# Row-maximum scores twelve steps ahead instead of ten, a thinner lead, and cosine-matrix differences made by GpSimd during the first attention layer

## The chip, the cores and the metric

The kernel runs on one core of one Trainium2 chip. The metric is the device time of one execution in microseconds (us); the profiles are those of single executions on the chip. Engines are named as the profile names them: PE is the matrix engine (PEld its weight loads), DVE the vector engine, ACT the scalar engine, POOL is GpSimd, SP the engine that issues the DMAs here. Every DMA of this kernel is issued on SP's queue, in program order.

## What is computed

Four layers on one sequence of 2048 tokens with 640 features, float32: sliding-window attention (32 heads of 20, window 256), a Fourier mixing layer, the same attention again, the same Fourier layer again. Each adds its result to its input.

```python
def _A_ref(x, wqkv, wo):                      # x is layer-normalised
    q, k, v = ...                             # x @ wqkv, 32 heads of 20
    scores = einsum("bhqd,bhkd->bhqk", q, k) * 20 ** -0.5
    mask = (i - j >= 0) & (i - j < 256)
    p = softmax(where(mask, scores, -1e9))
    return concat(p @ v) @ wo
def _B_ref(x, Cr, Ci, Wr, Wi):                # x is layer-normalised
    a, b = x @ Wr.T, x @ Wi.T
    return Cr @ a - Ci @ b
x = x + A(norm(x)); x = x + B(norm(x)); x = x + A(norm(x)); x = x + B(norm(x))
```

The layers are called first attention, first Fourier, second attention, second Fourier below. Cr and Ci are the 2048 x 2048 cosine and sine matrices.

## The kernel before, in words

**Precision.** Most float32 products are made of three reduced-precision ones: each operand is cut into a high part (a copy by ACT) and a low part (source minus high part, by DVE or POOL), `split` at L224 and `cut_job` at L216.

**Attention, the heads loop (`heads`, L606).** The heads are taken as 8 quads of 4 heads; a quad has 16 blocks of 128 queries. That makes 128 steps, preceded by LEAD more. In the step numbered `step` the loop does three things for three different places:

- at s = step + LEAD, the scores of one query block with up to three key blocks, two heads at a time (`s_head`, matmul at L631). DVE adds the mask and takes the row maximum in one instruction (L636), into `mc`. Every fourth block, `m_rows` (L641) turns the maxima (L644), ACT negates them (L647), and two DMAs write them as rows 60 and 124 of `qp` (L649).
- at t = step, the same scores transposed with that extra row (`t_pair`, L659), so that PE delivers score minus maximum; ACT takes the exponential (L669), POOL clears the corners outside the window (`t_mask`, L675 and L679).
- at v = step - 1, probabilities times values (`pv`, L694), copied out at L701. The values carry a column of ones, so row 0 of each head's output is the sum; `finish` (L705) posts the DMA of the sums (L711), of the output (L712), the reciprocal on DVE (L714) and its store (L717), each some ticks later. A tick is half a step; the three delays are `at`, (2, 9, 11) before quad 7.

S and T scores share four PSUM banks before step -1, six after, handed out by `borrow`. A bank is free again once DVE (S) or ACT (T) has read it.

**What fills PE in the heads loop.** `fill(n)` runs about n rounds of other work. A round is one `yield 1` of `lockstep` (L244): two matmuls of 64 rows that run at once. First comes `project` (L568): chunks 2 to 9 of the q/k projection, 60 rounds each, 15 per half of a pair of 512-token blocks. While `self.lead` is true (step < -2) a chunk takes all four blocks at once in four banks (role "f", 6, 7, 4, 5), else two blocks in two banks (role "m", 6 and 7). A half ends with a small DVE read of its banks (L263). Finished blocks are copied out by ACT (L544) and cut by POOL jobs (L552, L211), stored (L524) and loaded again as `qp` and `kp` of a later quad (`pack`, L594) at due times counted in s. Before step -1 both halves of a step call `fill`, afterwards only the first. n is at least FIRST in the lead, RATE = 4 later. When the last chunk has begun its second half, `prepare(2)` (L927) loads the first outputs for the output projection; when the projection is over, `prepare(4)` (L944) posts loads of x into `big` (L952), and `partials` (L954) does 14 blocks of 18 rounds at LATE = 9 per step, as soon as the first set of outputs has been loaded, scaled (L892) and cut. Its first three parts need the sums of quads 0 to 5. A block ends with a DVE addition of the x that was loaded (L978).

**Lanes.** `job(lane, ...)` puts small instructions into a queue for ACT, DVE or POOL; each tick takes one from each lane (two in the lead). `flush(key)` issues those of a key at once.

**Fourier, the sequence part.** A Strassen-like scheme needs, of the first quarter (sb 0, part 0) of the matrices, three quarters-of-columns p, q, ... and three differences of them per row block j (8 blocks): q - p for the units "a1"/"a2", "b"/"b7" and "g". `load_to` (L1249) loads 1024 columns, `cut_to` (L1298) makes the difference (L1325 on DVE; L1336 on DVE, L1288 for the two "b7" units; L1345 on DVE for j < 3, else POOL) and cuts the operands; `seq` issues the matmuls (L1416). In the first Fourier layer `keep` (L1275) also stores each difference to `c_d` in HBM; in the second, `sums_kept` is true: it loads the difference (L1255, L1267) in place of the other half and makes none. These units begin while the last output blocks of the attention layer still run (`after_heads`).

## Time and the profile before

| | us |
|---|---|
| three runs | 2186.35, 2188.07, 2188.04 (median 2188.04) |
| the profiled execution, its own time | 2187.93 |
| its span, first to last instruction | 2186.2 |
| heads of the first attention, first S matmul to last T matmul | 125.0 to 528.8 |
| heads of the second attention | 1216.9 to 1617.8 |
| first Fourier, sequence matmuls (L1416) | 541.7 to 973.3 |
| second Fourier, sequence matmuls | 1628.8 to 2051.3 |

The groups of instructions by line give busy time and the mean of one instruction; the table of stretches gives busy time of each engine in stretches cut at chosen instants, with granted PE clock, share of the DMA engines' time and GB/s. In the profile a matmul's duration is longer than the distance between two starts, since matmuls overlap: what one costs is read from the starts.

### The profile page before, as it was taken

What the parts mean: (1) busy time and instruction counts of PE and PEld (TensorE: products, weight loads), DVE (VectorE), ACT (ScalarE), POOL (GpSimd) and SP (SyncE); (2) the same over time, 40 slices, a digit from 0 to 9 for tenths busy, and PEclk for the clock granted to TensorE, in tenths of its full rate; (3) what the DMA queues carried; (4) which work ended last, traced back from release to release, by engine and by line L of the source; (5) the groups of instructions that cost most, each with busy time, mean ns of one, the idle gap of its engine ahead of it and who ended that gap; (6) DMA issues with size and microseconds to landing.
All of it is one profiled execution on the core that took longest, in us unless ns stands there. A gap on an engine that the chain in (4) does not pass through costs nothing.

```text
span 2186.2 us, 48927 instructions
## 1 busy us (share of the span) xinstructions
PE 2118.1 (97%) x17872; PEld 1783.2 (82%) x17872; DVE 1603.7 (73%) x3931; ACT 1140.5 (52%) x2125; POOL 958.0 (44%) x1562
## 2 busy tenths in 40 slices
PE   7999999988999999999999999999899999999999
PEld 7987777677878888889999877776778888888899
DVE  6358888886897868786661588888767968677676
ACT  3117777656554545452341177777565645445332
POOL 3037776765614222322430377767655033231324
PEclk9999999999999999999999999999999999999999
DMA  5546666785555354656645556567855454546653
GB/s 183 175 157 190 198 180 215 211 224 169 202 192 189 127 183 141 214 177 207 207 156 167 162 186 200 181 212 226 216 161 182 140 182 132 174 152 208 222 165 125
DMA packets 227089, 398.40 MB, mean 182 GB/s; under 512 B 39969, under 2 KB 86561, under 8 KB 226849
## 3 DMA queue, kind: packets, MB, share of 16 engines
q1 hardware_dynamic: 226848, 395.28, 57.3%
q8 instruction: 141, 2.31, 0.5%
q14 instruction: 100, 0.81, 0.1%
HBM read 273.94 MB, written 120.06 MB: 180 GB/s over the span
## 4 chain that ended last, share of the span: by engine, by line
PE 78%; DVE 7%; DMA 5%; ACT 4%; issue 3%; POOL 2%; SPq 1%; ACTq 0%; DVEq 0%; POOLq 0%
PE banks L1416 29%; PE banks L239 15%; PE banks L257 12%; PE banks L694 6%; PE banks L659 5%; PE banks L1704 5%; PE banks L631 5%; DMA qp<-qk_d 2%; DVE banks L636 1%; ACT pt L669 1%; DMA x_d<-x 1%; PE banks L341 1%; DMA kp<-qk_d 1%; ACT big L1039 1%; DVE qp L232 1%
## 5 line engine op out<-in xcount | busy, mean ns | idle before, releaser
L636 DVE CUSTOM_DVE_ANT_0 banks<-banks,mask 128x384 f32<-128x384 f32 (+2 forms) x1024 | 527.6, 557 | 123.0 <-PE banks L631 99.9
L669 ACT ACTIVATE pt<-banks 128x768 f32<-128x768 f32 (+2 forms) x512 | 393.8, 772 | 168.7 <-PE banks L659 55.2
L675 POOL TENSOR_SCALAR_AFFINE_SELECT pt<-pt 128x256 f32<-128x256 f32 x512 | 213.3, 417 | 213.8 <-ACT pt L669 192.0
L257 PE MATMUL banks<-big,wc 64*128 64x512 f32 x1920 | 271.1, 394 | 0.4 <-DVE pt L442 0.4
L659 PE MATMUL banks<-qp,kp 61*128 61x384 f32 (+2 forms) x1024 | 210.2, 381 | 22.8 <-DVE mc L636 17.4
L694 PE MATMUL banks<-pt,vq 128*32 128x128 f32 x5760 | 211.6, 278 | 3.5 <-ACT pt L669 3.4
L631 PE MATMUL banks<-kp,qp 60*128 60x384 f32 (+2 forms) x1024 | 205.5, 347 | 6.7 <-DVE mc L636 3.1
L257 PEld LDWEIGHTS banks<-big,wc 64*128 64x128 f32 x1920 | 186.8, 185 | 22.6 <-ACT x L544 1.5
L679 POOL TENSOR_SCALAR_AFFINE_SELECT pt<-pt 128x256 f32<-128x256 f32 x448 | 193.8, 433 | 0.0
L226 ACT ACTIVATE qp<-pt 128x512 fp32r<-128x512 f32 (+1 forms) x200 | 123.2, 625 | 128.1 <-DVE pt L1347 51.7
L232 DVE TENSOR_TENSOR qp<-pt,qp 128x512 fp32r<-128x512 f32 (+1 forms) x198 | 156.6, 798 | 42.1 <-ACT qp L226 40.5
L694 PEld LDWEIGHTS banks<-pt,vq 128*32 128x32 f32 x5760 | 142.4, 110 | 51.5 <-issue 35.3
L659 PEld LDWEIGHTS banks<-qp,kp 61*128 61x128 f32 x1024 | 108.0, 184 | 87.3 <-DVE mc L636 65.2
L1416 PE MATMUL banks<-qp,big 128*128 128x512 f32 x648 | 152.9, 390 | 0.0
L631 PEld LDWEIGHTS banks<-kp,qp 60*128 60x128 f32 x1024 | 123.6, 186 | 31.9 <-DVE mc L636 16.4
L1345 POOL TENSOR_TENSOR pt<-pt,pt 128x512 f32<-128x512 f32 x32 | 47.2, 1475 | 231.4 <-DMA pt<-c 173.4
L226 ACT ACTIVATE c<-pt 128x512 fp32r<-128x512 f32 x146 | 90.4, 625 | 111.1 <-POOL pt L1325 57.1
L636 DVE DVE_READ_ACCUMULATOR2_ANT mc<- 128x1 f32 x1024 | 145.0, 142 | 0.0
L1416 PEld LDWEIGHTS banks<-qp,big 128*128 128x128 f32 x648 | 120.8, 188 | 24.2
L232 DVE TENSOR_TENSOR c<-pt,c 128x512 fp32r<-128x512 f32 x144 | 113.8, 793 | 26.9 <-ACT c L226 24.4
L1416 PE MATMUL banks<-qp,xc 128*128 128x512 f32 x480 | 117.4, 391 | 4.3 <-DVE xc L232 2.8
L552 POOL CAST c<-x 128x512 fp32r<-128x512 f32 x64 | 38.9, 611 | 166.5 <-ACT x L544 162.3
(253 smaller groups left out, 4479.9 us busy)
## 6 DMA issues: line engine op xcount, KB each, us to landing
pt<-c SPq DMA_DIRECT2D x166, 512.0 KB
qk_d<-c SPq DMA_DIRECT2D x80, 512.0 KB
kp<-qk_d SPq DMA_DIRECT2D x384, 80.0 KB
qp<-qk_d SPq DMA_DIRECT2D x384, 80.0 KB
kp<-u_d SPq DMA_DIRECT2D x32, 640.0 KB
o_d<-ou SPq DMA_DIRECT2D x64, 256.0 KB
x_d<-x SPq DMA_DIRECT2D x48, 320.0 KB
v_d<-pt SPq DMA_DIRECT2D x16, 768.0 KB
```

The lines of the kernel that those rows point to most:

```text
L226: nc.scalar.activation(hi, src, AF.Copy, scale=-1.0 if neg else 1.0)
L232: (eng or nc.vector).tensor_tensor(out=lo, in0=src, in1=hi.bitcast(F32), op=OP.subtract)
L239: self.nc.tensor.matmul(p, x, y, start=n == 0, stop=n == last)
L257: self.nc.tensor.matmul(ps[a], x[r], y[r], start=half + i == 0, stop=half == 1 and i == n - 1, skip_group_check=True)
L631: nc.tensor.matmul(p, qp[quad % 2][b:b + 60, z, qb * P:(qb + 1) * P], kp[quad % 2][b:b + 60, z, k0 * P:(qb + 1) * P], start=True, stop=True)
L636: nc.vector.tensor_tensor_reduce(out=p, in0=p, in1=self.mask[:, 384 - n * P:], scale=1.0, scalar=NEG, op0=OP.add, op1=OP.max, accum_out=mc ...
L659: nc.tensor.matmul(self.banks[:, banks[e], :n * P], kp[quad % 2][b:b + 61, z, kb * P:(kb + 1) * P], qp[quad % 2][b:b + 61, z, kb * P:(kb + ...
L669: nc.scalar.activation(pt[quad, kb][:, 2 * z:2 * z + 2, :n * P], self.banks[:, b0:b1 + 1, :n * P], AF.Exp, scale=SCALE)
L675: nc.gpsimd.affine_select(out=t[:, :, 0:P], in_=t[:, :, 0:P], pattern=[[0, 2], [1, P]], compare_op=OP.is_ge, fill=0.0, base=0, channel_mul ...
L679: nc.gpsimd.affine_select(out=t[:, :, 256:384], in_=t[:, :, 256:384], pattern=[[0, 2], [-1, P]], compare_op=OP.is_gt, fill=0.0, base=0, ch ...
L694: nc.tensor.matmul(self.banks[32 * h:32 * h + 32, bank, :P], vq[:, 96 * (kb % 4) + 21 * h:96 * (kb % 4) + 21 * h + 32], t[:, h, (qb - kb) ...
L1416: nc.tensor.matmul(self.banks[:, bk, :], p, b[q], start=start and m == 0, stop=stop and last and m == 2, skip_group_check=True)
```

## The change

Six edits. LEAD goes from 10 to 12 and FIRST from 7 to 5. In the projection only the first chunk of the lead takes four blocks at once. `differences_at`, called once a step in the first attention only (`self.ready == 0`), works through the 8 row blocks in turns of ten steps: in steps 0, 1, 2 of a turn three loads of 128 x 512 into the three `rr` tiles, in step 3 six POOL jobs of 128 x 256 that make the three differences in place, in step 7 the stores to `c_d` (at ticks 0, 2 and 4). The first Fourier layer then always loads the kept differences, as the second did; `keep`, its stores, `sums_kept` and the difference instructions of that quarter go. The delays in `finish` become (2, 12, 14) before quad 7, apart from the first block of quad 5. The staged cuts of the unit "b7" lose their first stage.

```diff
-LEAD = 10
+LEAD = 12
...
-FIRST = 7
+TURN = 10
+FIRST = 5
...
     def project(self):
         for c in range(2, NCH):
-            lead = self.lead
+            lead = self.lead and c == 2
...
+    def differences_at(self, step):
+
+        j, at = divmod(step, TURN)
+        if not (0 <= j < NB // 2 and self.ready == 0):
+            return
+        c = self.rr
+        if at < 3:
+            self.nc.sync.dma_start(c[at], self.a["c"][0, 0, j][:, at * 512:(at + 1) * 512])
+        elif at == 3:
+            for out, x, y in ((0, 1, 0), (1, 2, 1), (2, 2, 0)):
+                for cs in (slice(0, 256), slice(256, 512)):
+                    self.job("pool", "cd", lambda out=out, x=x, y=y, cs=cs: self.nc.gpsimd.tensor_tensor(
+                        out=c[out][:, cs], in0=c[x][:, cs], in1=c[y][:, cs], op=OP.subtract))
+        elif at == 7:
+            self.flush("cd")
+            for k in range(3):
+                self.post(2 * k, lambda k=k: self.nc.sync.dma_start(self.cd[k, j], c[k]))
...
-            at = (2, 9, 11) if quad < NQ - 1 else (1, 5, 6)
+            at = (1, 5, 6) if quad == NQ - 1 else (2, 9, 11) if (quad, bk) == (NQ - 3, 0) else (2, 12, 14)
...
             self.wide, self.lead, self.tiled = step + LEAD > steps, step < -2, step < steps - 1
+            self.differences_at(step)
...
-                self.post(3, lambda u=u: self.staged(u, 0, nc.vector))
-                self.post(6, lambda u=u: self.staged(u, 1))
-                self.post(9, lambda u=u: self.staged(u, 2))
+                self.post(6, lambda u=u: self.staged(u, 0))
+                self.post(9, lambda u=u: self.staged(u, 1))
...
     def kept_sum(self, u):
-        return self.sums_kept and self.order[u][:2] == (0, 0)
-
-    def keep(self, u, t):
-
-        sb, part, ph, j = self.order[u]
-        if not self.sums_kept and sb + part == 0:
-            kind = {"a1": 0, "b": 1, "b7": 1, "g": 2}[ph]
-            self.keeping.append(lambda: self.nc.sync.dma_start(self.cd[kind, j], t))
+        return self.order[u][:2] == (0, 0)
...
             if ph in ("a", "a1"):
-                eng = nc.vector if ph == "a1" else nc.gpsimd
-                if not self.kept_sum(u):
-                    eng.tensor_tensor(out=t1, in0=q, in1=p, op=OP.subtract)
-                    if ph == "a1":
-                        self.keep(u, t1)
+                if ph == "a":
+                    nc.gpsimd.tensor_tensor(out=t1, in0=q, in1=p, op=OP.subtract)
...
                 cut(q)
-                eng = nc.vector if self.order[u][:2] == (0, 0) and j < 3 else nc.gpsimd
                 if self.kept_sum(u):
                     t1, p = p, t1
                 else:
-                    eng.tensor_tensor(out=t1, in0=p, in1=t1, op=OP.subtract)
-                    self.keep(u, t1)
+                    nc.gpsimd.tensor_tensor(out=t1, in0=p, in1=t1, op=OP.subtract)
...
-        self.ready, self.hid, self.sums_kept = 8, False, True
+        self.ready, self.hid = 8, False
```

More of the change, by code (lines that the diff above doesn't have):

```diff
@@ L95, in __init__ @@
         self.cd = dram.tile([3, NB // 2, P, 512], F32, name="c_d")
-        self.sums_kept = False
         self.xs = [dram.tile([S, D], F32, name=f"x_d{i}") for i in range(3)]
@@ L1218, in take_fourier @@
         self.acc = {}
-        self.leaving, self.keeping = [], []
+        self.leaving = []
     def take_rest(self):
@@ L1272, in kept_sum, with staged @@
     def kept_sum(self, u):
-        return self.sums_kept and self.order[u][:2] == (0, 0)
-    def keep(self, u, t):
-        sb, part, ph, j = self.order[u]
-        if not self.sums_kept and sb + part == 0:
-            kind = {"a1": 0, "b": 1, "b7": 1, "g": 2}[ph]
-            self.keeping.append(lambda: self.nc.sync.dma_start(self.cd[kind, j], t))
-    def staged(self, u, stage, eng=None):
+        return self.order[u][:2] == (0, 0)
+    def staged(self, u, stage):
         j, out = self.order[u][3], self.cut_of.setdefault(u, [])
         p, q = cuts(self.raw_of[u], 512)
-        if stage == 0:
-            if not self.kept_sum(u):
-                eng.tensor_tensor(out=p, in0=q, in1=p, op=OP.subtract)
-                self.keep(u, p)
-            return
         c = self.ring.popleft()
         self.ring.append(c)
-        self.split(c[0], c[1], (q, p)[stage - 1])
+        self.split(c[0], c[1], (q, p)[stage])
         out.append(c)
-        if stage == 1:
+        if stage == 0:
             self.kept[j] = c
@@ L1307, in cut_to @@
                 if j:
-                    self.staged(u, 0, nc.gpsimd)
+                    self.staged(u, 0)
                     self.staged(u, 1)
-                    self.staged(u, 2)
                 continue
@@ L1322, in cut_to @@
             if ph in ("a", "a1"):
-                eng = nc.vector if ph == "a1" else nc.gpsimd
-                if not self.kept_sum(u):
-                    eng.tensor_tensor(out=t1, in0=q, in1=p, op=OP.subtract)
-                    if ph == "a1":
-                        self.keep(u, t1)
+                if ph == "a":
+                    nc.gpsimd.tensor_tensor(out=t1, in0=q, in1=p, op=OP.subtract)
                 src = [p] + ([t1] if ph == "a" else [])
@@ L1336, in cut_to @@
                     nc.vector.tensor_tensor(out=p, in0=q, in1=p, op=OP.subtract)
-                    self.keep(u, p)
                 src = [q, p]
@@ L1386, in seq @@
         sb, part, ph, j = self.order[n]
-        for f in self.keeping:
-            f()
-        self.keeping.clear()
         self.load_to(n + 3 + (ph == "a1" and len(self.raws) > 5))
```

## The prediction

> **What bounds the kernel now.** I read the page first, then the table of stretches cut at the stage borders, first attention and first Fourier beside their twins, then the groups and the timeline of the stages that the change touches.
>
> ```profile
> PE 2118.1 (97%) x17872; PEld 1783.2 (82%) x17872; DVE 1603.7 (73%) x3931; ACT 1140.5 (52%) x2125; POOL 958.0 (44%) x1562
> ...
> 125.00:160.80 35.80, 35.41 (x314) 28.86 (x313) 22.99 (x85) 5.60 (x12) 14.75 (x22) 1.00 0.46 149
> 160.80:412.90 252.10, 247.68 (x3491) 188.03 (x3489) 209.95 (x787) 184.21 (x335) 184.18 (x422) 1.00 0.64 196
> 412.90:427.80 14.90, 13.27 (x167) 8.52 (x163) 12.40 (x45) 8.70 (x19) 12.11 (x26) 0.81 0.67 213
> 427.80:501.20 73.40, 65.79 (x1011) 54.48 (x1007) 59.10 (x199) 42.47 (x76) 44.17 (x96) 0.99 0.79 218
> 501.20:541.70 40.50, 35.73 (x509) 29.93 (x504) 22.41 (x45) 26.83 (x52) 24.77 (x48) 1.00 0.53 159
> 541.70:670.40 128.70, 120.65 (x558) 97.45 (x557) 114.67 (x243) 71.92 (x146) 45.73 (x49) 0.99 0.59 194
> 670.40:973.30 302.90, 301.91 (x1330) 249.24 (x1330) 235.21 (x330) 159.02 (x297) 87.83 (x60) 1.00 0.52 168
> 1216.90:1252.10 35.20, 35.20 (x313) 30.00 (x313) 23.02 (x85) 5.60 (x12) 14.71 (x22) 1.00 0.46 152
> 1252.10:1504.30 252.20, 247.73 (x3495) 187.72 (x3491) 210.05 (x787) 184.41 (x336) 184.44 (x422) 1.00 0.63 197
> 1504.30:1517.50 13.20, 11.58 (x165) 7.43 (x161) 11.83 (x43) 8.56 (x19) 11.21 (x24) 1.00 0.81 247
> 1517.50:1590.40 72.90, 65.23 (x1009) 53.96 (x1009) 59.56 (x201) 42.53 (x76) 44.88 (x99) 1.00 0.82 216
> 1590.40:1628.80 38.40, 35.77 (x508) 29.96 (x505) 21.45 (x43) 26.87 (x52) 24.31 (x48) 1.00 0.47 146
> 1628.80:1748.40 119.60, 116.81 (x558) 98.78 (x557) 102.34 (x232) 74.43 (x150) 37.99 (x44) 0.99 0.52 166
> 1748.40:2051.30 302.90, 301.81 (x1330) 249.12 (x1329) 231.32 (x326) 157.45 (x292) 85.95 (x59) 1.00 0.51 167
> ```
>
> Columns of a stretch: length, busy time (and instructions) of PE, PEld, DVE, ACT, POOL, then granted clock, DMA share, GB/s. The seven stretches of a layer pair are the lead, steps 0 to 91 with projection, steps 92 to 96, steps 97 to 117, the rest up to the first sequence matmul, the first stretch of the Fourier sequence part and its remainder. PE sets the lead and the loop; DVE is close behind in the loop (209.95 of 252.10). The twins agree in the loop and in the remainder (302.90 both), and differ in the start of the Fourier part: 128.70 against 119.60. That pair is the best witness here, because the second Fourier layer already runs the code that the first one gets.
>
> **The change part by part.** The sum is made against the profiled execution's 2187.93, which is the median of the runs (2188.04) but for 0.1.
>
> *The lead.* How it is spent, from the timeline of PE:
>
> ```profile
> 138.87 0.34 PE L631 MATMUL banks<-kp,qp 60*128 60x384 f32 x2
> 139.05 1.77 PE L257 MATMUL banks<-big,wc 64*128 64x512 f32 x14
> 140.65 0.34 PE L631 MATMUL banks<-kp,qp 60*128 60x384 f32 x2
> ...
> L636 DVE CUSTOM_DVE_ANT_0 banks<-banks,mask 128x384 f32<-128x384 f32 x30 | 16.2, 583 | 7.7 <-PE banks L631 7.7
> ...
> L544 ACT ACTIVATE x<-banks 128x512 f32<-128x512 f32 x8 | 4.3, 595 | 27.7 <-PE banks L257 15.7 <-PE banks L631 12.0
> ```
>
> Fourteen matmuls, 7 rounds, take 140.65 - 139.05 = 1.60, so a round is 0.229, and a pair of S matmuls 0.18. A step of the lead is now 15 rounds and two pairs, 3.79; with FIRST = 5 it is 10 rounds and two pairs, 2.65. (Five divides a half of 15 into three fills; the due times ask for at most 4.8 rounds per step.) Eight steps of 3.79 become ten of 2.65: 30.3 to 26.5, a gain of 3.8; steps -2 and -1 and the two transposes of maxima stay. DVE needs 4 x 0.58 = 2.3 of a 2.65 us step, so it doesn't take over, but it is near. Against the gain stands the two-bank form of the second chunk: the next pair of blocks must wait in the same banks for ACT's copies (0.595 each), and each half for DVE's small read, which queues behind two reductions. There are three such borders in the new lead, which no T or PV covers there; I bound them by 0 and 2.2 (one copy for 0.6 and its start, twice most of a reduction), and take 1.0. Per attention -2.8, together **-5.6**.
>
> *Where the 20 rounds go.* The lead now does 115 rounds instead of 135. At RATE 4, with halves of 15 taken as 4, 4, 4, 3, the remaining 345 rounds fill 92 steps; 365 fill 97.
>
> ```profile
> L257 PE MATMUL banks<-big,wc x22: 386/392/394, 404.8 to 411.3; 64*128 64x512 f32 x22
> L257 PE MATMUL banks<-big,big x18: 299/306/465, 428.6 to 430.0; 64*128 64x320 f32 x18
> ```
>
> The rows show the last projection matmul (step 91) at 411.3 and the first of the output projection (step 97) at 428.6: five steps with no fill, waiting for the outputs of quad 5's first block, the block whose early reciprocal the change keeps. They run at 13.20 / 5 = 2.64 a step, since DVE is busy 11.83 of 13.20; steps with projection take 252.20 / 92 = 2.74. So 20 rounds, 4.6 us of PE, move under DVE's cover for 5 x 0.1 = 0.5 an attention, **+1.0**. If that cover were not there, they would cost 4.6 each and the lead would be worth nothing.
>
> *The end of S.* S ends at step 116 instead of 118. From step 118 on a step is shorter:
>
> ```profile
> 1590.40:1611.20 20.80, 19.62 (x329) 15.79 (x325) 9.47 (x18) 15.86 (x30) 16.23 (x34) 1.00 0.42 128
> ```
>
> 20.80 / 7 = 2.97 against 72.90 / 21 = 3.47, though some of that average is single waits. Two steps at -0.3: **-1.2** for both attentions (0 to -2).
>
> *Loads in quad 7.* PE's waits in the two output stretches (first attention, then second), and a load of x by the chain of waits:
>
> ```profile
> PE banks L631 <- DMA kp<-qk_d: 1.0, 1, 1.0
> ...
> PE banks L631 <- DMA qp<-qk_d: 2.0, 1, 2.0
> ...
> 1589.56 3.97 DMA big<-x_d
> ```
>
> The first S of quad 7 waits for its operands, issued at steps 96 to 99 behind the first outputs and stores that crowd SP's queue. With LEAD 12 they go out at 94 to 97, ahead of the output loads of step 98. I take half, **-1.5** (-3.0 to 0). The other way goes the load of x: `prepare(4)` is posted when projection ends, at step 92 now, at 97 then. I count the jobs of the POOL lane to the first set of outputs as ready one step later, so block 0 runs in steps 98 and 99, and its addition on DVE (L978) is due about 6 us after the issue. Landing takes 3.97 plus SP's backlog; behind the waiting addition stand the reductions of S, and PE behind them. **+1.0** (0 to +6).
>
> *The clock.* In the five empty steps the first attention shows a granted clock of 0.81 and 14.90 us, its twin 1.00 and 13.20; steps 97 to 117 add 0.5. At most -2.2 if filled steps keep the clock; the twin had the same empty steps at full clock, so I take half, **-1.1**. The Trainium skill ("TensorE: Matmul & The Clock Gate", "What's actually happening") says that an idle window of about 3.4 us halves the clock, on a window that runs free of the kernel. That would explain why one of two equal stretches fell to half; by that rule alone the whole 2.2 is gained and the sum is 1.1 lower.
>
> *First Fourier.* What goes, from the stretch 541.7 to 670.4 (two DVE groups, one POOL group) and the stores:
>
> ```profile
> L1336 DVE TENSOR_TENSOR pt<-pt 128x512 f32<-128x512 f32 x6 | 4.1, 685 | 0.0
> ...
> L1345 DVE TENSOR_TENSOR pt<-pt,pt 128x512 f32<-128x512 f32 x3 | 2.1, 686 | 0.0
> ...
> L1345 POOL TENSOR_TENSOR pt<-pt,pt 128x512 f32<-128x512 f32 x2 | 3.6, 1804 | 5.4 <-DVE c L232 5.4
> ...
> L1280 SPq DMA_DIRECT2D c_d<-pt x18: 319/326/423, 539.4 to 663.0; - x18
> ```
>
> Removed are 24 differences and 24 stores; the loaded bytes stay, in other pieces. PE there is idle 128.70 - 120.65 = 8.0 against 2.8 in the twin. The twin differs by 9.1 in this stretch and by 2.1 in the one before it, where the first differences are made and one ACT wait falls that need not belong. I take **-10.0** (-9.1 to -11.2).
>
> *GpSimd in the first attention.* POOL's groups in the loop, one step of it, and DVE's wait for the sums:
>
> ```profile
> L675 POOL TENSOR_SCALAR_AFFINE_SELECT pt<-pt 128x256 f32<-128x256 f32 x153 | 62.2, 406 | 59.6 <-ACT pt L669 55.5 <-PE banks L694 2.6 <-PE banks L659 0.9
> L211 POOL TENSOR_TENSOR c<-x,c 128x256 fp32r<-128x256 f32 x40 | 29.6, 739 | 0.0
> ...
> 259.25 0.41 POOL L675 TENSOR_SCALAR_AFFINE_SELECT pt<-pt 128x256 f32<-128x256 f32 x1
> ...
> 261.11 0.86 PE L694 MATMUL banks<-pt,vq 128*32 128x128 f32 x24
> ...
> DVE rc L714 <- DMA sm<-ou: 0.2, 1, 0.2
> ```
>
> 48 subtractions of the form of L211 are 48 x 0.739 = 35.5 us, over 80 steps in which POOL is idle 27% (59 us). But they come six in three steps: 4.4 us against 3 x 0.74 = 2.2 idle, so POOL falls up to 2.2 behind and catches up in the other seven. The mask ends at 259.66 and the last third of PV that needs it starts near 261.7: a margin of 2.0. The projection's own POOL jobs (six every eight steps) share the lane, one job a tick, so two groups in a row add up; I take **+1.0** (0 to +6: 0.8 a turn). The 48 DMAs are 16 us of SP (0.33 each by L1280) in 219, and about 58 GB/s beside 196; the kernel moves 247 in the stretch at 1504. Their loads wait for stores three steps back; the stores wait for POOL, with the loads of later quads behind them, which are needed some five steps later. The later reciprocals I cost at nothing: DVE waits 0.2 for the sums in the whole loop (last row), and only quad 5's first block feeds a wait.
>
> The Trainium skill ("SBUF — State Buffer", "SBUF: two separate sides") has a rule against this part: GpSimd and a DVE operation with two SBUF inputs exclude each other for a whole instruction. The reductions (0.583) read PSUM and one SBUF operand, so by the rule only DVE's few weight cuts would wait, at most 10 x 0.74 = 7.4 us of DVE, and the sum would be up to 7 higher; no run here shows it for these.
>
> Sum: -5.6 + 1.0 - 1.2 - 1.5 + 1.0 - 1.1 - 10.0 + 1.0 = -16.4, so 2187.9 - 16.4 = **2171.5**.
>
> **The rivals.**
> - *Only the Fourier part pays.* The borders in the lead, DVE in steps 92 to 96 and the wait for x eat the heads' gain: -10 + 1 gives **2179**. For it: DVE has only 0.35 us a step to spare in the new lead. Against it: PE is the only full engine there.
> - *Everything pays.* No bubbles (-7.6 for the lead), +1.0, -2.0, -3.0, -2.2, -11.2, no charge for POOL: -25 gives **2163**.
> - *The differences don't leave the bound.* If the twins differ for another reason (their loads, the clock), only the heads' -6.4 with POOL's and part of the 9.1 remain: **2180**. Against it: the twin runs the very code.
> - *Slower: POOL becomes the bound of steps 3 to 6 of every turn.* PV waits for the masks behind the subtractions. With all 35.5 us on the path it is 2171.5 - 1 + 35.5 = **2206**. It decides once the delay exceeds the margin of 2.0 by more than 17.4 / 8 = 2.2 us a turn, twice the backlog that I count.
>
> **How the numbers follow.** Forecast 0.50, only Fourier 0.20, everything 0.12, differences 0.08, slower 0.10. All but the last are faster; 0.2% (4.4 us, about what a measurement tells from no change) is missed by the upper ends of the second and fourth, 0.06 together: faster 0.84, same 0.06, slower 0.10. The range 2162 to 2184 holds the first four with their bounds; the forecast's own is 2166 to 2177.
>
> **What would show it.** The lead (first S to first T matmul) at 32 to 34 instead of 35.2 to 35.8. Projection matmuls up to step 96 and at most one or two steps without fill. In the first Fourier stretch about 119.6 to 121, with no difference on DVE or POOL. Steps 3 to 6 of a turn in the first attention within 0.2 of the second's; if its steps 0 to 91 are over 6 longer than the twin's, POOL's cost is wrong. PE waits at quad 7's start shorter; a wait of L978 for the load of x near step 99 if that term is larger. A clock below 1 in the filled steps would show that the empty ones didn't cause it.

## The result and the profile after

The changed kernel takes 2210.74 us (median of 4 runs, 2210.48 to 2211.21) against 2187.19 (4 runs, 2186.24 to 2188.07): ratio 1.0111, 95% interval 1.0097 to 1.0126. It is 23.6 us slower; the prediction said 16.4 faster. The profiled execution took 2210.48.

The page's busy line and the table of stretches of the changed kernel, cut at the same borders as before (lead, steps 0 to 91, 92 to 96, 97 to 117, the rest, first stretch of the Fourier part; the second attention below):

```profile
PE 2123.2 (96%) x17872; PEld 1787.0 (81%) x17872; DVE 1587.6 (72%) x3913; ACT 1140.6 (52%) x2125; POOL 976.7 (44%) x1604
...
123.70:158.70 35.00, 32.98 (x282) 25.95 (x281) 27.38 (x101) 4.38 (x10) 12.30 (x18) 1.00 0.52 168
158.70:438.10 279.40, 258.36 (x3497) 193.33 (x3494) 215.21 (x784) 183.60 (x334) 213.03 (x467) 0.96 0.69 214
438.10:452.90 14.80, 13.81 (x204) 10.45 (x200) 12.39 (x45) 9.67 (x20) 12.03 (x24) 1.00 0.84 254
452.90:531.90 79.00, 66.00 (x985) 53.52 (x981) 56.25 (x186) 43.47 (x81) 46.27 (x102) 0.96 0.77 216
531.90:570.60 38.70, 36.41 (x520) 31.13 (x521) 19.67 (x43) 26.59 (x50) 25.52 (x50) 1.00 0.48 148
570.60:689.40 118.80, 115.90 (x559) 97.66 (x558) 102.49 (x232) 74.40 (x151) 37.39 (x44) 1.00 0.51 169
...
1234.50:1268.90 34.40, 32.78 (x282) 25.89 (x281) 27.40 (x101) 4.38 (x10) 12.30 (x18) 1.00 0.53 168
1268.90:1520.40 251.50, 246.78 (x3495) 187.17 (x3493) 210.06 (x784) 183.49 (x334) 182.58 (x419) 1.00 0.62 191
1520.40:1534.20 13.80, 13.50 (x202) 10.33 (x198) 12.14 (x44) 9.63 (x20) 11.94 (x24) 1.00 0.82 233
1534.20:1613.50 79.30, 67.51 (x985) 54.81 (x981) 56.35 (x186) 43.51 (x81) 46.44 (x103) 0.94 0.81 212
```

The first Fourier layer gave what it should: 118.8 against 128.7. Two stretches cost far more than that. Steps 0 to 91 of the first attention take 279.4 against 252.1, while the second attention, which makes no differences, takes 251.5. Steps 97 to 117 take 79.0 and 79.3 against 73.4 and 72.9, in both attentions. POOL is busier by its subtractions (213.03 against 184.18) and still idle for a quarter of the stretch.

**Steps 0 to 91.** PE's waits there, before (4.3 us in all):

```profile
PE banks L659 <- DVE mc L636: 3.4, 10, 0.6
PE banks L659 <- DMA qp<-qk_d: 0.9, 3, 0.4
```

A row gives who waits for whom, the sum in us, how often, and the longest. PE's two largest in the changed kernel, then two of POOL's:

```profile
PE banks L712 <- POOL pt L693: 8.1, 5, 2.5
PE banks L649 <- DVE mc L654: 4.6, 2, 4.3
```

```profile
...
POOL rr L617 <- DMA rr<-c: 9.3, 6, 3.4
POOL rr L617 <- DMA kp<-qk_d: 9.0, 2, 5.1
```

PE waits for POOL, for which it had no wait before, and for DVE up to 4.3 us at a time, where 0.6 was the longest. The first chain, in POOL's timeline, PE's and SP's:

```profile
289.23 0.72 POOL L617 TENSOR_TENSOR rr<-rr,rr 128x256 f32<-128x256 f32 x1 [5.10 <-DMA kp<-qk_d]
289.91 0.41 POOL L693 TENSOR_SCALAR_AFFINE_SELECT pt<-pt 128x256 f32<-128x256 f32 x1
```

```profile
290.37 0.41 PE L712 MATMUL banks<-pt,vq 128*32 128x128 f32 x4 [2.53 <-POOL pt L693]
```

```profile
285.81 0.40 SPq L613 DMA_DIRECT2D rr<-c  x1
```

A subtraction (L617) stood 5.10 us in POOL's in-order queue for its second block, whose load SP issued only at 285.81 (its row names a packed load that signals on a semaphore for which the subtraction also waits). The masks stood behind it, and PE's probabilities times values (L712) behind the masks. The second chain, in DVE's timeline, POOL's at the same time, and PE's:

```profile
332.56 5.10 DVE L211 TENSOR_TENSOR wc<-x,wc 128x384 fp32r<-128x384 f32 x1
337.58 0.55 DVE L654 CUSTOM_DVE_ANT_0 banks<-banks,mask 128x384 f32<-128x384 f32 x1
```

```profile
332.42 0.74 POOL L211 TENSOR_TENSOR c<-x,c 128x256 fp32r<-128x256 f32 x1
333.11 0.40 POOL L693 TENSOR_SCALAR_AFFINE_SELECT pt<-pt 128x256 f32<-128x256 f32 x1
...
336.52 0.72 POOL L211 TENSOR_TENSOR c<-x,c 128x256 fp32r<-128x256 f32 x1
```

```profile
333.62 0.34 PE L677 MATMUL banks<-qp,kp 61*128 61x384 f32 x2
338.25 0.69 PE L649 MATMUL banks<-kp,qp 60*128 60x384 f32 x2 [4.29 <-DVE mc L654]
```

A low part of a weight cut, 0.64 us on average before, took 5.10. It began while POOL worked off a backlog without a gap, and it ended 0.4 us after POOL's last instruction (336.52 + 0.72 = 337.24). The nine instructions that POOL started meanwhile are masks and pieces of the projection; no difference is among them. The reductions of S stood behind it on DVE, their banks stayed full, and PE stopped. PE's stop cut off the exponentials, hence the masks, and that is how POOL ran dry at last.

The longer stalls have an echo. Windows around a PV stall of 1.7 us that ended at 228.8, granted clock in the third column from the right:

```profile
222.00:230.20 8.20, 6.50 (x87) 4.85 (x87) 5.00 (x17) 5.46 (x10) 3.73 (x10) 1.00 0.81 211
230.20:233.60 3.40, 2.93 (x30) 1.78 (x30) 2.25 (x9) 1.50 (x3) 1.89 (x4) 0.51 0.66 157
233.60:242.00 8.40, 8.40 (x115) 6.38 (x119) 6.76 (x26) 5.78 (x10) 8.40 (x19) 1.00 0.49 156
```

For 3.4 us PE has half its clock and starts 30 matmuls where the next rate (115 in 8.4 us) would give 47. Steps 0 to 91 hold four such stretches of 3.4 us and one of 6.8. In these 20.4 us PE is busy for 17.7, so the half clock costs some 9 us (an estimate: half of the busy time), next to 15.7 of added waits (all rows of PE's waits in these steps sum to 20.0, against 4.3). The Trainium skill ("TensorE: Matmul & The Clock Gate", "What's actually happening") has the clock halved after an idle window of about 3.4 us. The trace agrees on the length, as every halved stretch in these steps is one or two such windows. It differs on the idle time: the halved stretches lie on one grid of 3.41 us, and each follows a stretch of the grid in which PE stood idle for 1.70 us or more, about half of it. With up to 1.47 us idle the next one kept the full clock. Idle time is not all that counts: at 1537.5 us the clock was halved after a stretch with 0.46 us of it.

**Steps 97 to 117.** One of PE's waits in the first attention, SP's timeline (issues of DMAs), and one window:

```profile
...
PE banks L649 <- DMA qp<-qk_d: 5.8, 2, 3.2
```

```profile
467.62 0.53 SPq L878 DMA_DIRECT2D x<-o_d  x1
468.58 0.52 SPq L884 DMA_DIRECT2D rr<-r_d  x1
469.60 0.35 SPq L735 DMA_DIRECT2D r_d<-rc  x1
470.44 0.39 SPq L524 DMA_DIRECT2D qk_d<-c  x1
471.97 0.34 SPq L971 DMA_DIRECT2D big<-x  x1
472.52 2.05 SPq L594 DMA_DIRECT2D qp<-qk_d  x3
...
478.53 1.24 SPq L594 DMA_DIRECT2D qp<-qk_d  x3
```

```profile
465.00:475.00 10.00, 9.77 (x163) 8.13 (x164) 7.30 (x29) 6.37 (x12) 6.83 (x17) 1.00 1.00 254
```

The DMA engines are full (1.00). Output loads, loads of x and the projection's last stores stand among the packed loads of quad 7's second block. Its scores at step 104 wait, and the step takes 11.4 us (11.1 in the second attention). Before, step 104 took 4.55, and step 106, where these scores ran then, 3.6.

### The profile page after: what moved, and what is told of

It is laid out like the page before. It is cut to its first block, busy times and chain, and to the rows that moved or that the text cites. A ratio compares the mean times of both kernels' runs of the same rounds, so it can differ in the third digit from the quotient of the medians.

```text
span 2208.8 us, 48983 instructions
## 1 busy us (share of the span) xinstructions
PE 2123.2 (96%) x17872; PEld 1787.0 (81%) x17872; DVE 1587.6 (72%) x3913; ACT 1140.6 (52%) x2125; POOL 976.7 (44%) x1604
## 4 chain that ended last, share of the span: by engine, by line
PE 70%; DMA 8%; DVE 8%; ACT 4%; issue 3%; POOL 3%; SPq 3%; ACTq 0%; DVEq 0%; POOLq 0%
PE banks L1412 29%; PE banks L239 13%; PE banks L257 10%; PE banks L1700 5%; PE banks L712 5%; PE banks L677 4%; PE banks L649 3%; DMA kp<-qk_d 2%; DVE banks L654 2%; DMA qp<-qk_d 1%; DMA kp<-u_d 1%; SPq L594 1%; ACT pt L687 1%; DMA qk_d<-c 1%; PE banks L341 1%
## 5 line engine op out<-in xcount | busy, mean ns | idle before, releaser
L693 POOL TENSOR_SCALAR_AFFINE_SELECT pt<-pt 128x256 f32<-128x256 f32 x512 | 212.4, 415 | 206.0 <-ACT pt L687 184.6
L257 PE MATMUL banks<-big,wc 64*128 64x512 f32 x1920 | 280.5, 399 | 3.6 <-DVE seen L263 1.9
L649 PE MATMUL banks<-kp,qp 60*128 60x384 f32 (+2 forms) x1024 | 207.8, 349 | 20.4 <-DMA qp<-qk_d 14.1
L712 PE MATMUL banks<-pt,vq 128*32 128x128 f32 x5760 | 215.6, 279 | 10.1 <-POOL pt L693 8.1
L712 PEld LDWEIGHTS banks<-pt,vq 128*32 128x32 f32 x5760 | 144.5, 110 | 62.4 <-issue 35.1
L697 POOL TENSOR_SCALAR_AFFINE_SELECT pt<-pt 128x256 f32<-128x256 f32 x448 | 190.2, 424 | 0.0
L232 DVE TENSOR_TENSOR c<-pt,c 128x512 fp32r<-128x512 f32 x146 | 118.4, 814 | 26.5 <-ACT c L226 24.1
L1329 POOL TENSOR_TENSOR pt<-pt 128x512 f32<-128x512 f32 x30 | 42.3, 1413 | 165.8 <-DMA pt<-c 141.9
```

The costliest lines, as they stand in the source:

```text
L232: (eng or nc.vector).tensor_tensor(out=lo, in0=src, in1=hi.bitcast(F32), op=OP.subtract)
L257: self.nc.tensor.matmul(ps[a], x[r], y[r], start=half + i == 0, stop=half == 1 and i == n - 1, skip_group_check=True)
L649: nc.tensor.matmul(p, qp[quad % 2][b:b + 60, z, qb * P:(qb + 1) * P], kp[quad % 2][b:b + 60, z, k0 * P:(qb + 1) * P], start=True, stop=True)
L693: nc.gpsimd.affine_select(out=t[:, :, 0:P], in_=t[:, :, 0:P], pattern=[[0, 2], [1, P]], compare_op=OP.is_ge, fill=0.0, base=0, channel_mul ...
L697: nc.gpsimd.affine_select(out=t[:, :, 256:384], in_=t[:, :, 256:384], pattern=[[0, 2], [-1, P]], compare_op=OP.is_gt, fill=0.0, base=0, ch ...
L712: nc.tensor.matmul(self.banks[32 * h:32 * h + 32, bank, :P], vq[:, 96 * (kb % 4) + 21 * h:96 * (kb % 4) + 21 * h + 32], t[:, h, (qb - kb) ...
```

## The experiments

All are compared with the kernel before, run beside them on the same chip (medians 2186.2 to 2188.3).

**One half of the change at a time.** The first keeps the differences and undoes the heads' edits (LEAD 10, FIRST 7, four blocks throughout the lead, old delays in `finish`); the second is the kernel before with the heads' edits.

> The differences alone: GpSimd makes them in the first attention's heads, the first Fourier layer reads them; lead, projection and reciprocals as before. Theory L (the subtraction stands in POOL's queue before its operands have landed, and the masks behind it hold PE): first attention 15 to 25 us longer than before in steps 0 to 91, first Fourier 11 to 12 shorter, no long step 104; about 2187.2 + 20 - 11.5 = 2196, 2190 to 2202. Rival H (the stalls of the first attention come from the heads' new timing, not from the differences): steps 0 to 91 within 3 us of before, about 2176.

> The heads' edits alone (LEAD 12, FIRST 5, four blocks only for the first chunk, later reciprocals); the differences are made in the first Fourier layer as before. Theory J (DMAs crowd at steps 97 to 101, where the end of the projection, the first output loads and the loads of quad 7 now meet): step 104 takes about 11 us in both attentions, each attention 5 to 8 us longer from step 92 on and 0.8 shorter in the lead; about 2187.2 + 10 = 2197, 2193 to 2202. Rival: the long step 104 is a late effect of the differences' DMAs; then it is about 3.5 us here and the kernel 2184 to 2187.

The differences alone took 2202.49 (ratio 1.0067, 1.0044 to 1.0090), the heads' edits alone 2195.11 (1.0036, 1.0023 to 1.0050): each half slows the kernel. With the differences alone steps 0 to 91 take 279.1; with the heads alone they take 251.5, and step 104 takes 10.1 and 11.8. So the two losses have separate causes, and their sum, 14.8 + 7.4, is near the change's 23.6.

Theory L came near in time, not in mechanism. PE's largest wait in steps 0 to 91 with the differences alone:

```profile
PE banks L677 <- DMA qp<-mt: 9.6, 6, 3.4
```

These are late rows of maxima; the masks held PE for only 3.3 us. With scores twelve steps ahead no such wait is left, the masks hold PE for 8.1, and the loss is the same 27 us.

**When the subtractions run, and their loads.**

```diff
-        elif at == 3:      # e3: subtractions two steps later, stores at 8, one tick apart
+        elif at == 5:
...
-        if at < 3:         # e4: loads in the first turn only
+        if at < 3 and j == 0:
```

> As after, with the subtractions put into POOL's lane at step 5 of a turn instead of 3, the stores at step 8 instead of 7. Theory L: POOL no longer waits for loads, most of the 21 us of quads 1 to 5 go; about 2210.7 - 17 = 2194, 2189 to 2199. Rival W (POOL's work, 4.4 us in three steps, is too much beside the masks): the work is as dense as before, 2207 to 2212.

> As after, but the three loads are made in the first turn alone: POOL subtracts and stores in all eight turns, what it stores is not the differences from the second turn on. Theory L: POOL never waits for a load after the first turn, quads 1 to 5 within 5 us of before; 2210.7 - 18 = 2193, 2187 to 2197. Rival W: the work is all there, 2206 to 2211.

Two steps more for the loads gave nothing: 2210.3 (1.0112, 1.0085 to 1.0139), steps 0 to 91 279.9. PE's waits for the masks went, others came. Without the loads it was 2197.39 and 263.8; what remained were two stalls, 3.9 us behind a DVE cut and 3.5 behind ACT. My theory of late loads alone had fallen.

**Loads and stores without subtractions; subtractions spread; DVE's cuts given to GpSimd.**

```diff
-                    self.job("pool", "cd", ...)   # e5: none; e6: one a step, TURN = 11
...
-                self.cut_job("dve", ("w", c), ...)
+                self.cut_job("pool", ("w", c), ...)   # e7
```

> The changed kernel without the six GpSimd subtractions of a turn: the three loads and three stores stay, so what is stored are blocks of the matrix and not their differences, and the first Fourier stage computes with those. The changed kernel took 2210.7 us, its first attention 279.4 us from step 0 to step 91 against 252.1 before. Theory P (GpSimd's work does the harm: where two subtractions fall into a step, its four masks of 0.40 us and two subtractions of 0.72 us are 3.0 us in a step of 2.7; it goes without a pause from instruction to instruction, DVE's subtraction of a weight cut, which reads two operands in SBUF as GpSimd's do, then waits up to 5.1 us, the masks come late, and TensorE's clock is halved for 7.7 us after each stall): steps 0 to 91 fall to 252 to 256, no cut on DVE lasts over 1.5 us, time 2184 to 2189. Rival D (the 0.8 MB of loads and stores a turn hold up SP's queue and the packed loads): steps 0 to 91 stay over 268, time over 2199.

> The changed kernel with one subtraction a step, at the third to the eighth step of a turn, a turn of 11 steps, and the stores at the ninth. Theory P: a step then has 1.6 us of masks, 0.72 of a subtraction and at most one piece of a projection's cut, 3.0 us at the worst and mostly 2.3; the backlog is shorter and rarer, and some stalls go: steps 0 to 91 at 258 to 270, time 2190 to 2202. Rival Q (GpSimd's in-order queue waits for the loads whatever the spacing, as SP issues them late): no gain, time over 2206, POOL's waits for the matrix's loads as in the changed kernel (9 us from 158 to 480).

> The changed kernel with the low parts of the projection's weights subtracted by GpSimd in place of DVE, as two halves each. Starvation (the 5.1 us cut of 332.6 was DVE waiting until GpSimd ran dry): no DVE subtraction is left that reads two operands in SBUF while the subtractions run, so that stall of 4.3 us and the halved clock behind it go, about 8 us, less what GpSimd's longer queue adds to late masks: 2199 to 2206. Rival (the long cut only shows a jam that has another cause): a stall of DVE or a wait for a mask takes its place, 2208 to 2216.

(The 7.7 us of halved clock in the first of these texts was misread; the windows show 3.4 or 6.8.) Theory P failed in part: without any subtraction the time is 2203.34 and steps 0 to 91 take 272.1, three quarters of the loss. No cut on DVE lasts over 1.1 us there; ACT waits, by the same kernel's waits of ACT in those steps:

```profile
ACT ou L714 <- DMA o_d<-ou: 15.5, 9, 2.9
...
ACT mt L660 <- DMA qp<-mt: 4.9, 7, 1.4
```

ACT may not write its next output or row of maxima until the last one has been stored, and these stores come late. PE in turn waits for ACT, in two rows that the kernel before doesn't have:

```profile
PE banks L644 <- ACT pt L682: 4.7, 15, 0.6
PE banks L672 <- ACT ou L714: 4.7, 8, 1.5
```

All of PE's waits come to 13.3 us there, 9.0 more than before, and 3.4 us at half clock are 1.7 more. The rest of the 20 us lies in matmuls that count as busy; how it is lost isn't shown. Spreading the subtractions gave 2208.02, with three stalls for masks of up to 5.6 us behind subtractions that waited for loads, so rival Q came nearer. With the cuts on GpSimd it was 2208.47. The long DVE cut was gone, as starvation demands, but masks took its place (11.0 us, longest 5.0), and the rival's time came. In the second attention, which makes no differences, the same edit gained: 33.5 us for the lead and 249.7 for steps 0 to 91, against 34.4 and 251.5.

**The parts one by one.** Loads alone (stores moved ahead of the heads), stores alone, both on buffers of their own, both with half the bytes, subtractions alone (loads in the first turn, stores ahead of the heads).

> The changed kernel without the subtractions and with the matrix's blocks loaded in the first turn only: 24 stores of 256 KB are left in the first attention's steps; what is stored isn't the differences. With loads and stores steps 0 to 91 took 272.1 us, with none of it (the heads' edits alone) 251.5. If the traffic itself or each place in SP's queue costs, half of it costs about half: 258 to 265, time 2194 to 2200. If it takes loads and stores together (SP held up by a load that waits for the store of the same buffer), 251 to 255 and 2190 to 2193.

> The changed kernel without the subtractions and with the stores moved ahead of the heads (of the first block, eight times over; what is stored isn't the differences): 24 loads of 256 KB are left in the first attention's steps, nothing waits for them, and a load waits for no store. By traffic or places in SP's queue alone, about half of the 20.6 us of loads and stores together: steps 0 to 91 at 258 to 265. If it takes both, 251 to 255. The time itself also holds what the moved stores cost ahead of the heads.

> The changed kernel without subtractions, with the 24 loads and the 24 stores of the first attention's steps on buffers of their own: loads go into two of the three, stores come from the third, so that no load waits for a store's landing; what is stored isn't the differences. Loads alone gave 255.2 us for steps 0 to 91, stores alone 254.1, both on the same buffers 272.1, none 251.5. Theory W (both cost more than their sum because each load waits in SP's queue for the store of its buffer, and packed loads, output stores and row loads wait behind it): 256 to 260. Rival T (12.6 MB are simply too much beside the heads' own traffic of 197 GB/s): 268 to 274.

> The changed kernel with the 48 subtractions in the steps, but with loads in the first turn only and the stores ahead of the heads; what is stored isn't the differences. Subtractions and stores together gave 263.8 us for steps 0 to 91, in two stalls. If GpSimd's work costs by itself (DVE's subtraction held until GpSimd pauses, and the halved clock after it), one or two stalls stay, at least one behind a DVE subtraction of over 4 us: 256 to 264. If it harms only by holding up the stores in SP's queue: 251 to 254.

> The changed kernel without subtractions, with 24 loads and 24 stores in the first attention's steps as before, but each of half a block (128 KB in place of 256); the full stores lie ahead of the heads; what is stored isn't the differences. Loads and stores of whole blocks gave 272.1 us for steps 0 to 91 (270.8 on buffers of their own), loads alone 255.2, stores alone 254.1. If the bytes do it (6.3 MB then, as with loads alone or stores alone): 253 to 258. If the 48 places in SP's queue do it (some 0.45 us each, 21 us, on a queue that issues for 187 of 250 us): 265 to 272.

| left in the first attention's steps | steps 0 to 91, us | time, us |
|---|---|---|
| nothing (heads' edits alone) | 251.5 | 2195.11 |
| 24 stores | 254.1 | 2188.04 |
| 24 loads | 255.2 | 2187.56 |
| loads and stores | 272.1 | 2203.34 |
| the same, buffers apart | 270.8 | 2202.80 |
| the same, half the bytes | 265.5 | 2196.00 |
| 48 subtractions | 257.9 | 2189.48 |
| subtractions and stores | 263.8 | 2197.39 |
| all (the change) | 279.4 | 2210.74 |

Each stretch is from one profile, each time a median. In the second attention, where these kernels do the same, steps 0 to 91 take 251.1 to 251.7, so 2.6 us are clear of that spread. The times don't compare with the first row's as the stretches do, since there the first Fourier layer still makes the differences. In the rows of the 24 loads, of half the bytes and of the 48 subtractions, stores of whole blocks lie ahead of the heads.

Loads cost 3.7, stores 2.6, both 20.6: neither costs half of what both do, as traffic or places alone would have it. Theory W falls, since separate buffers change 1.3 us, and rival T has its range. Half the bytes in as many transfers take away 6.6: at the edge of the range for places in SP's queue, and far from that for bytes (253 to 258). The subtractions alone cost 6.4, and nearly all of it is one stall. This was expected if GpSimd's work costs by itself. DVE's timeline of that kernel:

```profile
317.86 4.84 DVE L211 TENSOR_TENSOR wc<-x,wc 128x384 fp32r<-128x384 f32 x1
322.63 0.55 DVE L669 CUSTOM_DVE_ANT_0 banks<-banks,mask 128x384 f32<-128x384 f32 x1
```

Here no load and no store of a difference is about, and the cut again ends only when POOL runs dry: nine POOL instructions start during it. PE loses 3.89 us, and from 321.7 on it has half its clock for 6.8. Four kernels have one cut each of 4.7 to 4.8 us (this one, the differences alone, later subtractions, first loads only), besides the change's 5.10. In all five POOL starts nine instructions during it without a gap, and the cut ends 0.4 us after the last.

**Another queue for loads and stores.**

```diff
-            self.nc.sync.dma_start(...)
+            self.nc.scalar.dma_start(...)
```

> As with the loads and stores on buffers of their own and no subtractions (steps 0 to 91 270.8 us), but the 24 loads and 24 stores of the first attention's steps are issued by ACT's queue in place of SP's; bytes and times in the program are the same; what is stored isn't the differences. Half the bytes in as many transfers still gave 265.5. If SP's queue, which then has 48 places of 0.45 us less, is what the steps wait for: 252 to 258 and 2188 to 2193, ACT bearing 21 us of issuing in its idle time. If the bytes on the DMA engines are, or ACT has no room either: 264 to 274.

A miss of both ranges: 2242.3 (1.0247, 1.0214 to 1.0280), steps 0 to 91 309.9. ACT's waits there:

```profile
ACT mt L660 <- DMA qp<-mt: 20.6, 13, 3.9
ACT ou L714 <- DMA o_d<-ou: 19.8, 10, 4.1
ACT ou L714 <- DMA qp<-qk_d: 9.3, 2, 5.2
```

The last row is odd, as an output copy needs no packed load. In the trace each transfer of these kernels signals on one of eight semaphores, taken in turn (240 or 241 transfers on each in the kernel before), and none is issued before the transfer eight places ahead of it has landed: all updates of a semaphore by one transfer lie ahead of the issue of the next one on it. ACT's queue shares the eight, so ACT itself stood still for SP's transfers. The run therefore doesn't settle bytes against places. It points to eight in flight as a limit of its own. So does SP's largest wait in the kernel with loads and stores on SP's queue, where packed loads wait for a block of the matrix that they don't need:

```profile
SPq L594 <- DMA rr<-c: 7.9, 12, 1.5
```

In the steps before, 434 transfers in 249.6 us (the starts of steps 0 and 91) at a mean of 3.56 us from issue to landing, the last update of the transfer's semaphore, are 6.2 in flight. With loads and stores, 473 at 3.79 us would be 7.2 if the steps kept that length. A queue that full is held up by each burst, which fits the jump from 3.7 and 2.6 to 20.6, and fits that half the bytes took only 6.6 of it. That is worked out, not tested: no run here allows more than eight. Nor do SP's waits for transfers grow as the loss does: they sum to 17.6 us with neither, 28.4 with loads alone and 32.7 with both.

**Step 104.** The heads' edits with FIRST 7, so that projection ends at step 83; and with the old reciprocals.

> The kernel before with the change's edits of the heads (scores twelve steps ahead, the lead projecting one chunk with all four blocks, later reciprocals), but with the old rate of 7 fills in the lead, so that 50 rounds more lie in the lead and the projection ends at step 83 in place of 96. With the rate of 5 it took 2195.1, and step 104 took 10.1 and 11.8 us, waiting for the seventh quad's packed loads. Theory X (the four loads of x, the last stores of the projection and the loads of the output projection, which all start when the projection ends, meet that quad's packed loads at steps 97 to 101): with the end 13 steps earlier step 104 takes under 4 us in both attentions, time 2180 to 2186. Rival (twelve steps ahead leave the packed loads too late by themselves): step 104 still over 8, time 2192 to 2198.

> The kernel before with scores twelve steps ahead and the lead projecting one chunk with all four blocks, but with the reciprocals at their old times. With the later ones (2195.1) five loads of the output projection, 1.3 MB, were issued within 4.5 us, between the loads of the seventh quad that step 104 then waited for 10.1 and 11.8 us. If the later reciprocals bunch them, the output's loads go out some steps earlier and apart and step 104 takes under 7 us: 2188 to 2191. If the later end of the projection (step 96) alone bunches them, step 104 stays at 9 to 12 us: 2193 to 2197.

With the earlier end step 104 takes 4.45 in both attentions and steps 97 to 117 take 70.2 in both: theory X's mechanism holds. Its time doesn't, at 2204.34 (1.0077, 1.0061 to 1.0093). The stretches of that kernel's lead and loop say why:

```profile
123.70:172.10 48.40, 45.82 (x380) 35.34 (x381) 27.31 (x102) 7.40 (x16) 20.24 (x30) 1.00 0.46 153
172.10:423.90 251.80, 244.89 (x3436) 184.47 (x3432) 210.66 (x786) 182.58 (x332) 182.47 (x420) 1.00 0.63 197
```

The 50 rounds cost each lead 13.4 us (48.4 against 35.0); steps 0 to 91 give nothing back (251.5 with FIRST 5), and steps 97 to 117 only 8 each. The old reciprocals gave 2192.72 (1.0026, 1.0013 to 1.0039) with step 104 at 11.5 and 11.3: the later ones aren't the cause. With scores twelve steps ahead, the late end of the projection is; a late end with ten steps was not run.

**A place for the differences.** In the value projection ahead of the heads POOL is idle. Five blocks there and three in the lead; all eight there; five there and three in the steps, one in 28 steps. The heads' edits are undone in all three.

> The kernel before with the differences kept, but made where GpSimd has no work: five of the eight blocks during the value projection ahead of the heads (80 to 124 us, GpSimd busy for 0.0 us, the DMA engines 0.54 to 0.58), three in the lead; nothing of them is left in the steps, and the edits of the heads are undone. If the harm in the first attention comes from the place alone (a step of 2.7 us in which GpSimd, SP's queue and DVE's bank hand-over have no room), steps 0 to 91 stay at 252, the first Fourier stage keeps its 12 us, and what is left is what 12.6 MB more of traffic cost ahead of the heads, 0 to 6 us: 2175 to 2182, under both kernels. Rival (the traffic costs wherever it is put, since 180 GB/s and 115 to 130 more come near the 300 GB/s that the slices show at most): 2184 to 2196, with a longer stretch ahead of the first exponential.

> The kernel before with the differences kept, and all eight blocks of them made during the value projection ahead of the heads, none in the lead or the steps. With five there and three in the lead the time was 2187.2: the stretch ahead of the first score was 0.8 us longer, the lead 8.2 us longer (one wait of 5.3 us of TensorE in it), steps 0 to 91 the same, the first Fourier stage 10.7 us shorter. If the lead's 8.2 us come of the three blocks put there, and the eight cost 1 to 3 us ahead of the heads, 2177 to 2182, below both kernels. Rival (three blocks more in the projection press on its own loads as they did in the lead): 2184 to 2190.

> The kernel before with the differences kept: five blocks made ahead of the heads, three in the steps, one in 28 steps, with one half-width subtraction in two steps and one load or store in two steps. All eight ahead of the heads gave 2183.1, with the first score 5.7 us later; five there cost 0.8. A block in the steps is 1.6 MB in 75 us, 21 GB/s. If that hides: steps 0 to 91 within 1 us of 252.1, first score at 125 to 127, first Fourier stage 10 to 12 us shorter, 2176 to 2181. If the steps pay for each subtraction: 2182 to 2188.

The first missed at 2187.20 (1.0004, 0.9989 to 1.0018): steps 0 to 91 at 252.5 and the Fourier gain were there, but the lead took 44.0, with one PE wait of 5.3 in it. All eight ahead of the heads took 2183.10 (0.9973, 0.9961 to 0.9984), faster than both kernels; this is the best version found. Its stretches (end of the projection, the lead, steps 0 to 91, first Fourier):

```profile
95.00:130.70 35.70, 35.70 (x228) 34.33 (x226) 5.10 (x9) 5.61 (x12) 11.66 (x9) 1.00 0.90 294
130.70:166.50 35.80, 35.41 (x313) 29.25 (x313) 24.02 (x85) 5.60 (x12) 18.76 (x25) 1.00 0.60 206
166.50:418.80 252.30, 247.87 (x3495) 188.09 (x3491) 209.96 (x787) 184.28 (x336) 184.20 (x422) 1.00 0.62 196
547.20:665.20 118.00, 115.57 (x557) 97.49 (x557) 101.48 (x230) 74.25 (x150) 37.04 (x44) 1.00 0.51 168
```

Lead and loop are as before and the Fourier stretch has its 10.7; the first score comes 5.7 later, with the DMA engines at 0.90. Three blocks spread thin over the steps came to 2184.98 (0.9989, 0.9975 to 1.0002), not to be told from no change; its profile has 253.7 in steps 0 to 91 and 77.0 in 97 to 117.

## Why the prediction was wrong

- **First Fourier, right.** -10.0 was predicted and -9.9 measured in its stretch. The stretch before it also fell, from 40.5 to 38.7, but not for the differences: it takes 38.8 with the heads' edits alone and 41.6 with the differences alone. The rival in which the differences don't leave the bound is out: with the differences alone the Fourier stretch takes 118.1.
- **GpSimd in the first attention, wrong: +1.0 predicted, +27.3 measured.** This step broke the forecast, in three places. I costed POOL's backlog by the masks' margin, as if POOL only computed; it also waits, and the masks stand behind a late load (8.1 us of PE waits). I bounded DVE's lock by the length of POOL's instructions, "at most 10 x 0.74 = 7.4 us of DVE", as DVE's time beside PE's path. It was one cut of 5.10 us that stopped PE for 4.29. And I costed the 48 transfers by SP's 16 us and by 58 GB/s, both of which seemed to have room. Loads and stores together cost 20.6 without any subtraction. My slower rival (2206) had the place but only part of the mechanism: POOL's 35.5 us didn't go on the path, stalls and half clocks did. That its time came near is luck. The half clock behind the stalls, some 9 us, had no term in the sum at all.
- **The rule of the Trainium skill** ("SBUF — State Buffer", "SBUF: two separate sides") holds in kind: with the cuts on GpSimd no long DVE instruction is left. As the prediction used it, the loser waits out one instruction. Measured, a waiting DVE instruction lost to nine in a row. And the cost was not DVE's time but PE's, for PE stopped with it.
- **Loads in quad 7, wrong in sign: -1.5 and +1.0 predicted, +12.0 measured over both attentions** (steps 97 to 117). I moved the packed loads earlier and the end of the projection later, and checked each against the outputs, not against one another. The later end puts stores, loads of x and output loads among the packed loads, and the DMA engines fill up. The wait that I named, of the addition for its x (L997 now), came once in the first attention, for 1.2 us.
- **The lead, mis-sized: -2.8 each predicted, -0.8 measured.** PE's timeline of the changed lead shows two of the bubbles:

```profile
150.19 1.91 PE L257 MATMUL banks<-big,wc 64*128 64x512 f32 x10 [0.57 <-ACT x L544]
...
155.90 0.50 PE L257 MATMUL banks<-big,wc 64*128 64x512 f32 x1 [0.96 <-DVE seen L263]
```

With another of 0.4, which was there before, these are 2.0 us of idle against 0.4 before. The rest is slower work, by a cause that stays open: 282 matmuls in 32.98 us, where the old rate (314 in 35.41) gives 31.8. The bubbles were to be 2.2 at most; in all the lead lost 3.0 of the 3.8 that the step times promised.
- **Moved rounds, clock, end of S.** The projection runs to step 96 at clock 1.00, as said. Steps 92 to 96 changed by -0.1 and +0.6, against -0.1 for both terms together, and that they fit is in part luck. Against the twin's 13.2 us at full clock, the filled steps took 1.6 and 0.6 more, where 0.5 was predicted, and the 1.6 that the clock gave back in the first attention covered it. In the five kernels with the old lead, the empty steps lost the clock in two of ten attentions, so half was too much to take. The earlier end of S gave 0.2 where 0.6 was predicted for an attention: steps 115 to 117 took 9.2 us against 9.5 in the first.

## What to carry to other kernels

A loop whose queues are nearly full has no room for work that an average calls hidden: cost an added stream by what stands behind it in each in-order queue and by the transfers in flight, and add the clock that a stall takes with it (here from 1.7 us on). Look for a stage where the engine and its queues are idle together before filling gaps of a busy one; the same differences cost 27 us in the loop and 5.7 ahead of it. When a load's issue and the end of another stage both move, put all transfers of the new moment on one list.

## What was not expected of the hardware

- A DVE instruction with two SBUF operands can starve behind gapless GpSimd work: 4.7 to 5.1 us for an instruction of 0.64, five times in five kernels, ended each time by GpSimd running dry. GpSimd's next mask then waited 4.1 to 4.8 us for an exponential: it ran dry because PE had stopped.
- PE stalls of 1.7 to 4.3 us, not only whole windows of 3.4, brought 3.4 or 6.8 us at half clock, and this echo was about 9 of the 27 us.
- Two streams of transfers that cost 2.6 and 3.7 us alone cost 20.6 together. The eight transfers in flight may be the limit; that is not shown.
